# First Q and K weight slices issued by GpSimd, and the first K tile split into a head of 128 tokens and a rest of 384

## The chip, the cores and the metric

The kernel runs on one core of one Trainium2 chip. The metric is the device time of one execution in microseconds (us). A core has five engines with queues of their own: PE (matmul), DVE (vector), ACT (scalar), POOL (GpSimd) and SP (sync, which here issues most DMAs). Each works through its queue in order and waits on semaphores that other engines, or landed DMAs, raise.

## The reference

A self-attention block and a bilinear gated feed-forward block read the same input x (2048 tokens of 512), and a gate of each token mixes the two results. Inputs and output are bf16.

```python
g = sigmoid((x * gate_w).sum(-1, keepdims=True))
q, k, v = split_heads(x @ wqkv)              # 32 heads of 16
p = softmax(q @ k.T * 16 ** -0.5)            # 2048 x 2048 for each head
a = merge_heads(p @ v) @ wo
b = ((x @ w_gate) * (x @ w_up)) @ w_down     # inner width 1376
out = g * a + (1 - g) * b
```

## The kernel before

The whole program is written out as straight code: about 21,000 instructions, no loops on the chip. While it is built, a small model of the engines (`K`, with durations and latencies written into the source) is run as an event simulation; what each model engine picks next becomes the fixed order of that engine's queue on the chip. The list `P.ops` holds the resulting operations with their dependences, and `P.emit` turns these into semaphore waits. A string of digits, `ORDER`, overrides some choices. The model's times set the order alone; on the chip each engine goes through its list as the semaphores allow.

Work is tiled by 512 tokens and by blocks of 128 features (four blocks `b`, each of 8 heads). A column matmul (`mm_col`, L422 to L429, profile line L427) takes 128 input features by 32 output features, on one of four column groups of the array, against 512 moving columns; a tile of 128 x 512 takes four steps over the features times four groups, sixteen matmuls, into one bank of PSUM (`ps[:, bank, :]`, eight banks of 512 columns). Banks 0 to 6 are handed out freely; bank 7 (`OB`) belongs to the PV product, the sum of probabilities times values, and before that to the six warm-up matmuls on zeros (L389).

What matters here is the start, in the order of the queues:

- Loads (`load`, L352 to L376, profile line L354). SP and ACT issue two pieces of the first 512 tokens of x each (`PT<-in_A_x`), then SP the Q weights of the first 128 features (`wq0`, into `wq`) and ACT the K weights of the same (`wk0`, into `wa`, whose first part is `wk`); each slice is 128 KB in runs of 256 bytes. SP goes on with the V weights (`wv`, also in `wa`, 512 KB) and with twelve transposing DMAs that bring the other 1536 tokens of x into `xT`.
- POOL first fills the columns of ones in `V0` (L411), the tails of the weight tiles (L412 to L414), zeros QE (L415, after the constant `sel` of DVE) and does one integer add (L416).
- PE transposes the four x pieces (tiles x0 to x3, L465); DVE (L477) and ACT (L475) copy them in turn into `xT`.
- PE then makes tile q00 (Q of the first 512 tokens, block 0) and tile k00 (K of the same), and the V tiles of 128 tokens each (`mk_v`).
- Evacuation: q00 goes to `QE` by DVE in two operations, L507 for the even heads and L510 for the odd ones, which waits for K's copy; k00 is copied to `KK` by ACT (L487); V tiles by DVE (L555).
- A score burst (`burst`, profile line L910) is up to four row matmuls, one unit each: 128 keys of one head against 512 queries. Its dependences are the banks, Q's evacuation and the K tile that holds its keys (L887).
- ACT takes the exponential of up to three banks at once (L1008). For up to 6 of the 16 key blocks DVE and POOL do a bit-level exponential instead (L1043, L1093). PE multiplies the results by V into bank 7 (`pv_pack`, L1143); the first pack of a group also waits for what `pv_rel[0]` names, the release of that bank, empty at the start (L789).

The lines that the change and the prediction touch:

```python
359  load("sp", "wq0", wq[:, :, 0:128], wcol(0, 128), lat=4500)
360  load("act", "wk0", wk[:, :, 0:128], wcol(D, D + 128), lat=4500)
361  load("sp", "wv", wv, wcol(2 * D, 3 * D), lat=5200)
427  r = pe.matmul(ps[32 * i : 32 * i + 32, bank, :], w, x_, start=s0, stop=s1,
428                tile_position=(0, 32 * i), skip_group_check=True)
484  dst = KK[:, b, ch * 512 : (ch + 1) * 512]
486  if (b, ch) == (0, 0):
487      K.task("act", [last], lambda a: a.activation(dst, ps[:, bank, :], ACT.Copy), ...)
491  x_ = lambda kt: xT[:, kt, ch * 512 : (ch + 1) * 512]
789  pv_rel = [[]]
887  part_deps.append(bank_rel[bank] + q_ready(m) + [ev_k[b, kt // 4]])
```

Of the kernel before, what the change touches and what calls it, by code (L numbers as in the profile page):

```python
# [14 lines left out]
ACT = mybir.ActivationFunctionType  # L15
# [237 lines left out]
S, D, H, Dh, F = 2048, 512, 32, 16, 1376  # L253
T, KD, NCH, NB, FT = 16, 4, 4, 4, 11
# [7 lines left out]
OB = 7  # L262
# [27 lines left out]
def _build(nc, A_x, A_wqkv, A_wo, W_gate, W_up, W_down, gate_w, out):  # L290
# [8 lines left out]
    with ExitStack() as stack:  # L299

        def sb(name, shape, dt):
            return stack.enter_context(nc.sbuf_tensor(name, shape, dt))

        xT = sb("xT", [128, KD, S], BF16)
        wa = sb("wa", [128, FT * 512], BF16)
        wk = wa[:, 0:2048].rearrange("p (k n) -> p k n", k=KD)
# [4 lines left out]
        wq = sb("wq", [128, KD, D], BF16)  # L311
# [4 lines left out]
        KK = sb("KK", [128, NB, S], BF16)  # L316
# [24 lines left out]
        ps = stack.enter_context(nc.psum_tensor("ps", [128, 8, 512], F32))  # L341
        xr = PT[:, NC - 4 : NC, :]

        P = _Plan()
        K = _Clock(P)
# [3 lines left out]
        wcol = lambda lo, hi: A_wqkv[:, lo:hi].rearrange("(kt p) n -> p kt n", p=128)  # L349
        ld = {}  # L350

        def load(eng, key, dst, src, deps=(), lat=2500.0, **kw):  # L352
            pr = kw.pop("prio", 5)
            K.task(eng, list(deps), lambda e: e.dma_start(dst, src, **kw), 480.0, lat, lambda o: None, pr, "d" + key, 16,  # L354
                   begun=lambda o: ld.__setitem__(key, o))

        for t in range(4):
            load(("sp", "act")[t % 2], f"x0{t}", xr[:, t, :], x2[t * 128 : (t + 1) * 128, :], lat=2900)
        load("sp", "wq0", wq[:, :, 0:128], wcol(0, 128), lat=4500)
        load("act", "wk0", wk[:, :, 0:128], wcol(D, D + 128), lat=4500)  # L360
        load("sp", "wv", wv, wcol(2 * D, 3 * D), lat=5200)
        t_x = {}
        for ch in range(1, NCH):
# [23 lines left out]
        for i in range(6):  # L387
            K.task("pe", lambda: [c["pt0"]] if "pt0" in c else None,
                   lambda pe: pe.matmul(ps[:, OB, :], PT[:, 0, 0:128], PT[:, 0, :], start=True, stop=True), 427.0, 630.0, None, 0,  # L389
                   begun=lambda o: pt_first.append(o), gate=(lambda: not any(tl.name[0] == "x" for tl in tiles)) if i > 4 else None)  # L390
# [28 lines left out]
        def wcols(w, kt, c0, rhs):  # L419
            return (w[:, kt, c0 : c0 + 128], rhs)  # L420

        def mm_col(pe, bank, piece, s0, s1):  # L422
            r = None
            lhs, rhs = piece
            for i in range(4):
                w, x_ = (lhs, rhs[i]) if isinstance(rhs, list) else (lhs[:, 32 * i : 32 * i + 32], rhs)
                r = pe.matmul(ps[32 * i : 32 * i + 32, bank, :], w, x_, start=s0, stop=s1,  # L427
                              tile_position=(0, 32 * i), skip_group_check=True)
            return r  # L429

        def mm_row(pe, bank, piece, q, s0, s1):
            lhs, rhs = piece
            return pe.matmul(ps[:, bank, :], lhs[32 * q : 32 * q + 32, :], rhs[32 * q : 32 * q + 32, :], start=s0, stop=s1,  # L433
                             tile_position=(32 * q, 0), skip_group_check=True)

        ev_x, ev_k, ev_v, ev_vs, ev_q, ev_z, ev_h, ev_ot = {}, {}, {}, {}, {}, {}, {}, {}
        last_k, last_v, last_z = {}, {}, {}
        bank_rel = {b_: [] for b_ in range(8)}
# [6 lines left out]
        def xdep(ch):  # L445
            if ch == 0:
                return [ev_x.get(t) for t in range(4)]
            return [ld.get(f"x{ch}{kt}") for kt in range(KD)]

        def have(l):  # L450
            return l if all(o is not None for o in l) else None

        def give(bank, ops, hard=-1e9):
            bank_rel[bank] = ops
            bank_hard[bank] = hard
            pool_free.append(bank)
            if bank in fill_bank:
                fill_bank.remove(bank)
                fill_n[0] -= 1
# [21 lines left out]
        def mk_k(b, ch, due):  # L481
            def evac(bank, last):
                last_k[b, ch] = last
                dst = KK[:, b, ch * 512 : (ch + 1) * 512]
                reg = lambda o: ev_k.__setitem__((b, ch), o)
                if (b, ch) == (0, 0):
                    K.task("act", [last], lambda a: a.activation(dst, ps[:, bank, :], ACT.Copy), 480.0, 610.0, lambda o: give(bank, [o]), 1, begun=reg)  # L487
                else:
                    K.task("dve", [last], lambda v: v.tensor_copy(dst, ps[:, bank, :]), 600.0, 690.0, lambda o: give(bank, [o]), 2, begun=reg)

            x_ = lambda kt: xT[:, kt, ch * 512 : (ch + 1) * 512]
            return _Tile(f"k{b}{ch}", [wcols(wk, kt, b * 128, x_(kt)) for kt in range(KD)],
                         lambda: have([ld.get("wk0" if b == 0 else "wk1")] + xdep(ch)), evac, due)

# [234 lines left out]
        for t in range(4):  # L729
            tiles.append(mk_x(t))  # L730
        tiles += [mk_q(0, 0, -9), mk_k(0, 0, -9)]
        for ch in range(4):
            if ch:
                tiles.append(mk_k(0, ch, 16 * ch - 16))
            tiles += [mk_v(t, 4 * t - 8) for t in range(4 * ch, 4 * ch + 4)]
        seq = []
        for b in range(1, NB):
            lo, hi = 128 * b - 64, 128 * b - 4
            seq += [(mk_q, (0, b), lo)] + [(mk_k, (b, ch), lo + (hi - lo) * (ch + 1) // 5) for ch in range(NCH)]
            if b == 1:  # L740
                seq += [(mk_z, (), hi)]
# [20 lines left out]
        def info(m):  # L762
            return m // 8, (m % 8) // 2, m % 2
# [22 lines left out]
        pv_last = {}  # L786
        pvm = [0]
        pv_open = [True]
        pv_rel = [[]]  # L789
        mode, second = [None], [False]  # L790
        scored_n = {}

        def q_ready(m):
            cq, b, p = info(m)
            d = ev_q.get((cq, b, p))
            return d if d and all(K.ready(o) for o in d) else None
# [64 lines left out]
        def burst(picks, late=False):  # L861
            part_deps = []
# [19 lines left out]
            for k_, (who, u) in enumerate(picks):  # L882
                m, kt, j = u
                cq, b, p = info(m)
                bank = abk.pop(0) if who == "a" else lone.pop(0)
                pool_free.remove(bank)
                part_deps.append(bank_rel[bank] + q_ready(m) + [ev_k[b, kt // 4]])  # L887
                todo.append((who, u, bank))
                (act_u if who == "a" else dve_u).remove(u)
                (act_out if who == "a" else dve_out)[0] += 1  # L890
                scored_n[m] = scored_n.get(m, 0) + 1

            qt = quarter({u[2] for _, u in picks})
            if qt is not None:
                tl, kq, q = qt
# [51 lines left out]
        def pe_issue(md, fn, deps, cost, done=None, share=None, add=0.0):  # L947
            sw = SWITCH if mode[0] not in (None, md) else SECOND if second[0] else 0.0
            second[0] = mode[0] not in (None, md)
            mode[0] = md  # L950
            cost, extra = cost + add, add
            if K.now < COLD:
                cost, extra = cost * 1.8, extra + 245.0
            o = K.issue("pe", fn, deps, cost + sw, MML + sw + extra, done)
            o.work = share or MM
            return o
# [335 lines left out]
        def fill_begin(tl):  # L1292
            got = sorted(avail("col"))
            tl.bank = min(got, key=lambda x: (x - 1 in got) + (x + 1 in got))
            pool_free.remove(tl.bank)
            fill_n[0] += 1
            return bank_rel[tl.bank]

        def fill_end(tl, o):
            if not tl.todo and tl.part is None:  # L1300
                tiles.remove(tl)
                fill_bank.add(tl.bank)
                tl.evac(tl.bank, o)

        def run_fill(tl):
            deps = tl.deps()
            if tl.bank is None:
                deps = deps + fill_begin(tl)
            k, n, bank = tl.todo.pop(0), len(tl.pieces), tl.bank
            fn = tl.pieces[k]  # L1310
            s0, s1 = not tl.begun, not tl.todo and tl.part is None
            tl.begun = True
            if tl.mode == "full":
                o = pe_issue(tl.mode, lambda pe: fn(pe, bank, s0, s1), deps, tl.cost)
            else:
                o = pe_issue(tl.mode, lambda pe: mm_col(pe, bank, fn, s0, s1), deps, tl.cost)
            if hasattr(tl, "mark"):
                tl.mark(tl, o)
            fill_end(tl, o)

        def pe_step():
# [47 lines left out]
            if code == "b":  # L1369
                burst(picks)  # L1370
            elif code == "l":
                burst(later, True)
            elif code in "xy":
                burst(other[code])
            elif code == "f":
                run_fill(tl)
            elif code == "p":
                pv_pack(pv)
            elif code == "s":
                solo(sl)  # L1380
# [120 lines left out]
        P.op("sp", lambda e: e.nop(), outs)  # L1501
        if False:
            print("model", K.now, {k: round(v) for k, v in K.busy.items()}, stat)
        P.ahead = {"pe": 60, "sp": 250}
        P.emit(nc, stack, False)

# [132 lines left out]
```

## Time and profile before

| what | value |
|---|---|
| three executions | 645.26, 645.44 and 648.53 us; median 645.44 |
| profiled execution | span 643.6 us from the first to the last instruction; its own time is not listed, so the span stands 1.8 us under the median |
| busy in the span | PE 99%, ACT 97%, DVE 94%, POOL 86% |
| granted TensorE clock | 1.000 |
| first column matmul of Q | at 6.87 us |
| first scores | at 9.79 us |
| first exponential | at 10.24 us |

How to read it: the chain of work that ended last, followed back from the last instruction, tells which waits set the end. An engine that is idle elsewhere costs nothing. Times in the rows are us from the start of the span. A DMA's row shows how long its issue took; when its data lands stands in the table of DMA issues.

### The profile page before, as it was taken

The numbers are of one execution on the slowest core, as the hardware profiler recorded it, in microseconds if no ns is written. First come the engines' busy times: TensorE is split into PE (matmuls) and PEld (weight loads), VectorE is DVE, ScalarE is ACT, GpSimd is POOL, SyncE is SP. The second block draws the span as 40 slices with busy tenths as digits, with TensorE's granted clock in tenths as the row PEclk, the third lists the DMA queues.
The fourth block names the chain that finished last, engine by engine and source line by source line (L and its number), as shares of the span: only waits on it lengthen the run. The fifth ranks groups of instructions, "written<-read, shape, count | busy, mean of one in ns | idle before, by whom it ended". The sixth has DMA issues, their size and how long they took to land.

```text
span 643.6 us, 21192 instructions
## 1 busy us (share of the span) xinstructions
PE 637.1 (99%) x8729; PEld 191.8 (30%) x8729; DVE 602.5 (94%) x1021; ACT 621.7 (97%) x753; POOL 553.6 (86%) x1431
## 2 busy tenths in 40 slices
PE   8999999999999999999999999999999999999997
PEld 3332322222223232222322222332222222322233
DVE  6999999999999999999998999999998999999986
ACT  5899999999999999999999999999999999999993
POOL 2669899998998999898889999988898999899882
PEclk9999999999999999999999999999999999999999
DMA  8930201000010100101010010100001010000101
GB/s 151 287 101 15 66 10 41 2 14 26 3 36 10 39 15 16 32 1 35 5 30 16 16 40 10 31 8 12 27 7 40 20 35 3 9 23 2 29 20 35
DMA packets 28658, 21.15 MB, mean 33 GB/s; under 512 B 16488, under 2 KB 24396, under 8 KB 28560
## 3 DMA queue, kind: packets, MB, share of 16 engines
q1 hardware_dynamic: 27600, 19.26, 11.7%
q8 instruction: 68, 1.11, 0.8%
q10 hardware_dynamic: 960, 0.52, 0.3%
q14 instruction: 30, 0.25, 0.1%
HBM read 11.63 MB, written 2.37 MB: 22 GB/s over the span
## 4 chain that ended last, share of the span: by engine, by line
PE 90%; ACT 9%; DMA 1%; DVE 0%; SPq 0%; issue 0%
PE ps L1143 32%; PE ps L427 28%; PE ps L910 26%; ACT PT L1008 9%; PE ps L433 3%; DMA wq<-in_A_wqkv_dram 1%; PE ps L1254 0%; SPq L354 0%; DVE QE L714 0%; PE ps L1446 0%; DVE fl L1441 0%; DVE cb L1451 0%
## 5 line engine op out<-in xcount | busy, mean ns | idle before, releaser
L1008 ACT ACTIVATE PT<-ps 128x1024 bf16<-128x1024 f32 (+2 forms) x743 | 615.8, 1005 | 5.2 <-PE ps L910 4.5
L1093 POOL INT64_ADD PT<-PT x1420 | 550.6, 408 | 75.1 <-DVE PT L1043 65.4
L1043 DVE TENSOR_SCALAR PT<-ps 128x512 int16<-128x512 f32 x728 | 471.3, 683 | 27.1 <-PE ps L910 15.4
L910 PE MATMUL ps<-QE,KK 32*128 32x512 bf16 x2048 | 245.0, 384 | 0.1
L1143 PE MATMUL ps<-PT,V 128*32 128x512 bf16 (+1 forms) x2048 | 232.5, 384 | 0.0
L1143 PE MATMUL ps<-PT,VS 128*32 128x512 f16 x1456 | 186.6, 383 | 0.0
L910 PEld LDWEIGHTS ps<-QE,KK 32*128 32x128 bf16 x2048 | 63.6, 91 | 230.0 <-ACT PT L1008 185.2
L1143 PEld LDWEIGHTS ps<-PT,V 128*32 128x32 bf16 x2048 | 57.7, 95 | 62.9 <-issue 49.4
L1143 PEld LDWEIGHTS ps<-PT,VS 128*32 128x32 bf16 x1456 | 45.6, 95 | 42.0 <-issue 26.6
L427 PE MATMUL ps<-xT,wg 128*32 128x512 bf16 x704 | 54.6, 383 | 0.0
L427 PE MATMUL ps<-xT,wu 128*32 128x512 bf16 x704 | 54.1, 383 | 0.0
L427 PE MATMUL ps<-wd,wa 128*32 128x512 bf16 x704 | 51.6, 382 | 0.0
L624 DVE TENSOR_TENSOR usb<-ps,omg 128x512 bf16<-128x512 f32 x44 | 29.9, 680 | 0.2
L651 DVE TENSOR_TENSOR wa<-ps,usb 128x512 bf16<-128x512 f32 x44 | 29.9, 680 | 0.1
L433 PE MATMUL ps<-wo,OT 32*128 32x512 bf16 x60 | 23.1, 384 | 0.2
L1240 DVE COPY oc<-ps 128x512 f32<-128x512 f32 x31 | 21.1, 679 | 0.0
L427 PEld LDWEIGHTS ps<-wd,wa 128*32 128x32 bf16 x704 | 14.7, 95 | 19.7 <-issue 11.9
L427 PE MATMUL ps<-xT,wa 128*32 128x512 bf16 x272 | 20.2, 382 | 0.0
L427 PE MATMUL ps<-xT,wq 128*32 128x512 bf16 x256 | 18.5, 382 | 1.4 <-DMA wq<-in_A_wqkv_dram 1.4
L427 PEld LDWEIGHTS ps<-xT,wu 128*32 128x32 bf16 x704 | 13.8, 95 | 18.9 <-issue 10.4
L427 PEld LDWEIGHTS ps<-xT,wg 128*32 128x32 bf16 x704 | 13.8, 95 | 18.7 <-issue 11.1
L427 PE MATMUL ps<-wa,xT 128*32 128x512 bf16 x256 | 17.1, 381 | 0.0
(74 smaller groups left out, 142.2 us busy)
## 6 DMA issues: line engine op xcount, KB each, us to landing
rb<-rscr SPq DMA_DIRECT2D x16, 256.0 KB
QE<-Qr SPq DMA_DIRECT2D x120, 16.0 KB, 1.8
oc<-oc SPq DMA_DIRECT2D x60, 32.0 KB, 1.9
out_dram<-ost SPq DMA_DIRECT2D x12, 128.0 KB, 1.7
wu<-in_B_w_up_dram SPq DMA_DIRECT2D x1, 1376.0 KB, 6.8
wg<-in_B_w_gate_dram SPq DMA_DIRECT2D x1, 1376.0 KB, 11.0
wd<-in_B_w_down_dram SPq DMA_DIRECT2D x1, 1280.0 KB, 14.3
wa<-in_A_wqkv_dram SPq DMA_DIRECT2D x1, 512.0 KB, 6.1
```

What stands on the lines that cost most here:

```text
L427: r = pe.matmul(ps[32 * i : 32 * i + 32, bank, :], w, x_, start=s0, stop=s1, tile_position=(0, 32 * i), skip_group_check=True)
L433: return pe.matmul(ps[:, bank, :], lhs[32 * q : 32 * q + 32, :], rhs[32 * q : 32 * q + 32, :], start=s0, stop=s1, tile_position=(32 * q, 0 ...
L624: return v.tensor_tensor(usb[:, st["s"], :], ps[:, bank, :], omg[:, cf, :], ALU.mult)
L651: return v.tensor_tensor(hT[:, f, :], ps[:, bank, :], usb[:, u_at[cf, f][0], :], ALU.mult)
L910: return lambda pe: pe.matmul(ps[:, bank, :], KK[32 * j : 32 * j + 32, b, kt * 128 : (kt + 1) * 128], QE[32 * j : 32 * j + 32, p, b, :], s ...
L1008: o = K.issue("act", lambda a: a.activation(PT[:, cs, :], ps[:, bs, :], ACT.Exp, scale=math.log(2.0) / 1024.0), deps, 63.0 + 427.0 * n, 17 ...
L1043: o = K.issue("dve", lambda v: v.tensor_scalar(PT[:, y, :].bitcast(I16), ps[:, bank, :], BIAS16, 0.0, ALU.add, ALU.max), [dep] + pt_rel[y] ...
L1093: return g.int64_add(PT[:, zl, :].bitcast(I64), PT[:, sl, :].bitcast(I64), w)
L1143: return lambda pe: pe.matmul(ps[32 * it.j : 32 * it.j + 32, OB, :], lhs, it.rhs, start=s0, stop=s1, tile_position=(0, 32 * it.j), skip_gr ...
L1240: K.task("dve", deps, lambda v: v.tensor_copy(oc[:, p, :], ps[:, OB, :]), 600.0, 690.0, done, 0)
```

## The change

The two weight slices are issued by POOL, as the first operations of its queue; SP and ACT run a no-op where they issued them. Sixteen column matmuls of 128 columns (`k_head`), ahead of q00 on PE, make K of the first 128 tokens in bank 7, and ACT copies it to `KK` (`head_out`), just ahead of its other K copy. They wait for `wk0` and the first x tile. Tile k00 then covers tokens 128 to 511 in columns 128 to 511 of its bank. Score units on the first 128 keys of block 0 wait for `head_out` instead of for the copy of k00, and the first PV pack waits for `head_out` too, for the bank. The model is not told of the head: the orders of all other operations stay as they are.

```diff
@@ -356,8 +356,10 @@
 
         for t in range(4):
             load(("sp", "act")[t % 2], f"x0{t}", xr[:, t, :], x2[t * 128 : (t + 1) * 128, :], lat=2900)
-        load("sp", "wq0", wq[:, :, 0:128], wcol(0, 128), lat=4500)
-        load("act", "wk0", wk[:, :, 0:128], wcol(D, D + 128), lat=4500)
+        for eng, key, dst, lo in (("sp", "wq0", wq, 0), ("act", "wk0", wk, D)):
+            first = P.op("pool", lambda e, dst=dst, lo=lo: e.dma_start(dst[:, :, 0:128], wcol(lo, lo + 128)), (), "d" + key, 16)
+            K.task(eng, [], lambda e: e.nop(), 480.0, 4500.0, None, 5,
+                   begun=lambda o, key=key, first=first: (setattr(first, "t1", o.t1), ld.__setitem__(key, first)))
         load("sp", "wv", wv, wcol(2 * D, 3 * D), lat=5200)
         t_x = {}
         for ch in range(1, NCH):
@@ -422,9 +424,10 @@
         def mm_col(pe, bank, piece, s0, s1):
             r = None
             lhs, rhs = piece
+            at = 0 if isinstance(rhs, list) else 512 - rhs.shape[1]
             for i in range(4):
                 w, x_ = (lhs, rhs[i]) if isinstance(rhs, list) else (lhs[:, 32 * i : 32 * i + 32], rhs)
-                r = pe.matmul(ps[32 * i : 32 * i + 32, bank, :], w, x_, start=s0, stop=s1,
+                r = pe.matmul(ps[32 * i : 32 * i + 32, bank, at:512], w, x_, start=s0, stop=s1,
                               tile_position=(0, 32 * i), skip_group_check=True)
             return r
 
@@ -433,6 +436,17 @@
             return pe.matmul(ps[:, bank, :], lhs[32 * q : 32 * q + 32, :], rhs[32 * q : 32 * q + 32, :], start=s0, stop=s1,
                              tile_position=(32 * q, 0), skip_group_check=True)
 
+        def k_head(pe):
+            r = None
+            for kt in range(KD):
+                for i in range(4):
+                    r = pe.matmul(ps[32 * i : 32 * i + 32, OB, 0:128], wk[:, kt, 32 * i : 32 * i + 32], xT[:, kt, 0:128], start=kt == 0, stop=kt == KD - 1,
+                                  tile_position=(0, 32 * i), skip_group_check=True)
+            return r
+
+        head = _Op("pe", k_head, [], "pe", 1)
+        head_out = _Op("act", lambda a: a.activation(KK[:, 0, 0:128], ps[:, OB, 0:128], ACT.Copy), [head], "act", 1)
+        k_first = {}
         ev_x, ev_k, ev_v, ev_vs, ev_q, ev_z, ev_h, ev_ot = {}, {}, {}, {}, {}, {}, {}, {}
         last_k, last_v, last_z = {}, {}, {}
         bank_rel = {b_: [] for b_ in range(8)}
@@ -484,11 +498,12 @@
                 dst = KK[:, b, ch * 512 : (ch + 1) * 512]
                 reg = lambda o: ev_k.__setitem__((b, ch), o)
                 if (b, ch) == (0, 0):
-                    K.task("act", [last], lambda a: a.activation(dst, ps[:, bank, :], ACT.Copy), 480.0, 610.0, lambda o: give(bank, [o]), 1, begun=reg)
+                    K.task("act", [last], lambda a: a.activation(dst[:, 128:512], ps[:, bank, 128:512], ACT.Copy), 480.0, 610.0, lambda o: give(bank, [o]), 1, begun=reg)
                 else:
                     K.task("dve", [last], lambda v: v.tensor_copy(dst, ps[:, bank, :]), 600.0, 690.0, lambda o: give(bank, [o]), 2, begun=reg)
 
-            x_ = lambda kt: xT[:, kt, ch * 512 : (ch + 1) * 512]
+            lo = 128 if (b, ch) == (0, 0) else 0
+            x_ = lambda kt: xT[:, kt, ch * 512 + lo : (ch + 1) * 512]
             return _Tile(f"k{b}{ch}", [wcols(wk, kt, b * 128, x_(kt)) for kt in range(KD)],
                          lambda: have([ld.get("wk0" if b == 0 else "wk1")] + xdep(ch)), evac, due)
 
@@ -786,7 +801,7 @@
         pv_last = {}
         pvm = [0]
         pv_open = [True]
-        pv_rel = [[]]
+        pv_rel = [[head_out]]
         mode, second = [None], [False]
         scored_n = {}
 
@@ -884,7 +899,7 @@
                 cq, b, p = info(m)
                 bank = abk.pop(0) if who == "a" else lone.pop(0)
                 pool_free.remove(bank)
-                part_deps.append(bank_rel[bank] + q_ready(m) + [ev_k[b, kt // 4]])
+                part_deps.append(bank_rel[bank] + q_ready(m) + [ev_k[b, kt // 4] if (b, kt) != (0, 0) else head_out])
                 todo.append((who, u, bank))
                 (act_u if who == "a" else dve_u).remove(u)
                 (act_out if who == "a" else dve_out)[0] += 1
@@ -1314,6 +1329,8 @@
                 o = pe_issue(tl.mode, lambda pe: fn(pe, bank, s0, s1), deps, tl.cost)
             else:
                 o = pe_issue(tl.mode, lambda pe: mm_col(pe, bank, fn, s0, s1), deps, tl.cost)
+            if tl.name in ("q00", "k00"):
+                k_first.setdefault(tl.name, o)
             if hasattr(tl, "mark"):
                 tl.mark(tl, o)
             fill_end(tl, o)
@@ -1501,6 +1518,12 @@
         P.op("sp", lambda e: e.nop(), outs)
         if False:
             print("model", K.now, {k: round(v) for k, v in K.busy.items()}, stat)
+        head.deps = [ld["wk0"], ev_x[0]]
+        P.ops.insert(P.ops.index(k_first["q00"]), head)
+        P.ops.insert(P.ops.index(ev_k[0, 0]), head_out)
+        P.nstream.clear()
+        for o in P.ops:
+            P.nstream[o.stream] = o.seq = P.nstream.get(o.stream, 0) + 1
         P.ahead = {"pe": 60, "sp": 250}
         P.emit(nc, stack, False)
```

## The prediction

> **What bounds the kernel now.** I read the page first (shares of the engines, the chain that ended last), then the chain in order of time over the first 16 us, then the timeline of that stretch engine by engine, and last the table of DMA issues of the first 30 us.
>
> ```profile
> span 643.6 us, 21192 instructions
> PE 637.1 (99%) x8729; PEld 191.8 (30%) x8729; DVE 602.5 (94%) x1021; ACT 621.7 (97%) x753; POOL 553.6 (86%) x1431
> PE 90%; ACT 9%; DMA 1%; DVE 0%; SPq 0%; issue 0%
> ```
>
> PE is busy for 99% of the span and holds 90% of the chain that ended last. The change touches one short place, the start, where the chain in order of time (start, us, what) reads:
>
> ```profile
> 1.66 5.08 DMA wq<-in_A_wqkv_dram
> 6.73 0.14 issue
> 6.87 2.99 PE ps L427 x52
> 9.86 0.33 PE ps L910 x4
> 10.19 1.62 PE ps L427 x28
> ```
>
> The kernel waits for the first Q weight slice, issued at 1.66 and landed at 6.73. From 6.87 on PE does 52 column matmuls, four score matmuls, and goes on without a pause. The timeline shows who stands where (start, us, engine, line, operation, count, [idle before it <- what ended that]):
>
> ```profile
> 0.73 0.58 POOL L411 MEMSET V<- 128x256 bf16 x2 [0.29 <-POOLq L1624]
> 0.73 0.88 SPq L354 DMA_DIRECT2D PT<-in_A_x_dram  x2
> 1.64 0.31 POOL L414 MEMSET wd<- 32x256 f32 x1
> 1.66 0.43 SPq L354 DMA_DIRECT2D wq<-in_A_wqkv_dram  x1
> 1.67 0.46 ACTq L354 DMA_DIRECT2D wa<-in_A_wqkv_dram  x1
> 2.13 0.51 SPq L354 DMA_DIRECT2D wa<-in_A_wqkv_dram  x1
> 3.61 1.66 PE L465 MATMUL ps<-idn,PT 128*128 128x128 bf16 x16
> 3.79 0.29 DVE L406 TENSOR_SCALAR sel<-sel,rb 128x128 f32<-128x128 f32 x1
> 4.13 1.38 POOL L415 MEMSET QE<- 128x1536 f32 x1 [2.18 <-DVE sel L406]
> 4.66 1.24 ACT L475 ACTIVATE xT<-ps 128x512 bf16<-128x512 bf16 x2 [1.01 <-PE ps L465]
> 5.11 0.38 PE L389 MATMUL ps<-PT 128*128 128x512 bf16 x1
> 6.84 0.58 PEld L427 LDWEIGHTS ps<-xT,wq 128*32 128x32 bf16 x16 [1.69 <-issue]
> 6.87 1.05 PE L427 MATMUL ps<-xT,wq 128*32 128x512 bf16 x16 [1.39 <-DMA wq<-in_A_wqkv_dram]
> 7.73 1.05 PE L427 MATMUL ps<-xT,wa 128*32 128x512 bf16 x16
> 8.59 1.26 PE L427 MATMUL ps<-wa,xT 128*32 128x512 bf16 x20
> 8.83 0.60 ACT L487 ACTIVATE KK<-ps 128x512 bf16<-128x512 f32 x1 [2.92 <-PE ps L427]
> 9.79 0.39 PE L910 MATMUL ps<-QE,KK 32*128 32x512 bf16 x4
> 10.24 3.06 ACT L1008 ACTIVATE PT<-ps 128x1536 bf16<-128x1536 f32 x4 [0.81 <-PE ps L910]
> 11.74 0.40 PE L910 MATMUL ps<-QE,KK 32*128 32x512 bf16 x4
> ```
>
> Three things to see. PE stands idle for 1.39 us before 6.87, for the wq slice and nothing else: the transposed x is complete at 4.66 + 1.24 = 5.90. The 16 matmuls of Q, the 16 of K and the 20 of V follow with starts 0.86 us apart per sixteen. And the first scores do not wait for K: K is in SBUF at 8.83 + 0.60 = 9.43, the scores start at 9.79, when the V matmuls ahead of them on PE end (8.59 + 1.26 = 9.85). Landing times (last number, us after the issue):
>
> ```profile
> wa<-in_A_wqkv_dram SPq DMA_DIRECT2D x1, 512.0 KB, 6.1
> PT<-in_A_x_dram SPq DMA_DIRECT2D x2, 128.0 KB, 2.8
> wq<-in_A_wqkv_dram SPq DMA_DIRECT2D x1, 128.0 KB, 5.1
> wa<-in_A_wqkv_dram ACTq DMA_DIRECT2D x1, 128.0 KB, 5.3
> ```
>
> So wq lands at 6.7, wk at about 7.0, wv (512 KB) at 2.13 + 6.1 = 8.23, just ahead of its use at 8.59.
>
> **Two weight issues move to POOL.** They stand first in its queue, at 0.73, where the memset of V stands now; SP and ACT each run a no-op where they issued. The trace has no DMA issued by POOL, so its price is bounded. Low end: it issues as SP does, 0.43 us each, the second starting at 1.16, and the data lands like a lightly queued x piece, 2.8 us later: wk at 4.0. High end: POOL gets to its descriptors only when DVE's constants are done (4.08, the sel row), with the full 5.3 us behind it: 9.4. I take the nearest row, the same slice issued by ACT: 1.16 + 5.3 = 6.46 for wk, and 0.73 + 5.1 = 5.83 for wq.
>
> [...]
>
> What the two issues push back on POOL: the ones in V (needed by the first copy of V), three memsets of weight tails, the zeroing of QE and the first integer add. Cover: POOL waits 2.18 us for sel before the QE memset, so issues of up to 1.09 us each move nothing. Behind that it is idle until the first real add:
>
> ```profile
> 10.12 0.68 DVE L555 CAST V<-ps 128x512 bf16<-128x512 f32 x1
> 13.53 0.77 POOL L1093 INT64_ADD PT<-PT  x2 [7.68 <-DVE PT L1043]
> ```
>
> Together 2.18 + 7.68 = 9.9 us for two issues. The ones are due at 10.12 and are written at 1.31 now, 8.8 us of slack. Only issues of over 4.4 us each would reach DVE, and then each further microsecond costs one.
>
> SP's later work comes 0.43 + 0.04 us earlier: wv issued at 1.66 lands at about 7.76 by its own 6.1 us, and the twelve DMA transposes of the rest of x move up with it. ACT's issue ends 0.46 us earlier, ahead of a table load that is done long before x is copied. Neither is on the path as it stands; wv becomes it if Q starts early.
>
> The x pieces now share the DMA engines with the weight slices from the start. How full those are:
>
> ```profile
> 2.00:3.00 1.00, 1.00 (x4) 0.30 (x2) 0.83 (x8) 0.84 (x1) 0.00 (x0) 1.00 0.89 253
> 3.00:4.00 1.00, 0.89 (x7) 0.42 (x6) 0.84 (x11) 0.64 (x2) 0.00 (x0) 1.00 1.00 311
> ```
>
> The last two columns are the share of the engines' time and GB/s. At 311 GB/s a 128 KB slice takes 0.42 us, so x comes 0 to 0.4 us later per slice that gets ahead of it; I take 0.2, and xT is complete at 6.1. That is hidden as long as wk lands later than that, as taken.
>
> **The K head.** Sixteen matmuls of 128 columns, ahead of Q on PE, waiting for wk and the first x tile. This is an added wait: behind it on PE stands everything, Q first, which before needed only wq. Columns are conserved (K's tile shrinks from 512 to 384), so the streaming time only moves; what is added is sixteen weight loads and their pace. Q's sixteen loads start within 0.58 us where PE was not yet limiting, 36 ns each: I take 0.58 us for the head. Low end 0, if wk lands before xT is complete and the head runs inside that wait; high end the present 0.86 us per sixteen.
>
> The narrower K tile: 0.86 x 128/512 = 0.22 us less on PE (low end 0 if weight loads set the pace).
>
> **The head's copy on ACT**: 128 columns, at most the 0.60 us of the present 512-column copy; K's remaining copy shrinks. ACT stands idle 2.92 us before K's copy and 0.81 before the first exponential. The copy runs under Q's matmuls: nothing, and at worst 0.6 less K's saving if the head ran so late that both copies meet.
>
> **Releasing the first scores on the head instead of on K**: nothing, for PE reaches them at 9.79 and K was there at 9.43. Behind them ACT has K's other copy ahead of the first exponential in its own queue anyway.
>
> **The values' bank**: the first PV pack now also waits for the head's copy. That comes at 14.24, the copy is over by about 8:
>
> ```profile
> 14.24 0.60 PE L1143 MATMUL ps<-PT,V 128*32 128x512 bf16 x7
> ```
>
> **The sum.** wk lands 6.46; PE starts 0.14 later, as now, 6.60; head 0.58: Q at 7.18 against 6.87, +0.31. K is 0.22 shorter: V at 8.68 against 8.59, +0.09, and wv at 7.76 is no hindrance. From there the same instructions in the same order, with PE 90% of the chain, so the shift carries to the end nearly one for one: span 643.7. The span lies 1.8 us under the median of 645.44, and nothing of the change lies outside it but the issue's start: 645.5. The three times span 645.26 to 648.53, 0.5%, so 0.5% (3.2 us) is about what a measurement can tell from no change.
>
> **Rivals.**
>
> *Weights early.* wk lands between 4.0 and 6.1; the head vanishes in the wait for x; Q starts at about 6.2. Then K ends at 6.2 + 0.86 + 0.64 = 7.7 and V starts when wv is there, 7.76: 0.83 us ahead of 8.59. Time 644.6. For it: PE's 1.39 us of idle is weight wait alone, and POOL could issue 0.9 us before SP does. Against it: the DMA engines are full from 2 to 4 us, so an earlier issue mostly reorders the same bytes.
>
> *Late descriptors.* DVE is 0.83 and 0.84 busy in the rows of 2 to 4 us, on the constants that end at 4.08. If POOL cannot write descriptors beside it, wk lands at 6.8 to 9.4; Q starts at wk + 0.72, which is 7.5 to 10.1, and V 0.4 to 3.0 us later than now: 645.9 to 648.5, middle 647. Against it: POOL's memsets at 0.73 to 1.95 ran beside busy DVE rows. [...]
>
> *A slow first DMA on POOL* (the other side). If POOL's first DMA carries a start-up of t before its first descriptor, Q moves by all of t: PE has no other work. From t = 3.1 us on the kernel is slower by over 0.5%. The wait would also let PE cool:
>
> ```profile
> L389 PE MATMUL ps<-PT x6: 379/634/634, 1.2 to 5.1; 128*128 128x512 bf16 x6
> ```
>
> These are the warm-up matmuls, 634 ns until 5 us of the span and 379 then. With t = 5 us and four microseconds at 634 instead of 379 ns (1.6 us lost), the time is 652. Against it: POOL's first integer add, at 5.66, starts without any start-up in the trace.
>
> *The change does nothing* falls within my forecast: the head and the narrower K cancel, and the weights land when the full DMA engines allow.
>
> **How the numbers follow.** Forecast as summed 0.45 (645.5, with 0.5 either way for x, head and copy); early weights 0.28; late descriptors 0.20; slow start 0.05; 0.02 for a median that falls on a run like the 648.53. The likeliest is 645.5. The range takes in the early case with its low end (644.6 less the 0.6 by which wv could come early, 644.0) and most of the late one (to 647.5), leaving out about 0.15. Only the slow start and a stray median are past +0.5%, for the late case ends at 3.0 us: slower 0.07; no case gives 3.2 us, the whole of the wait being 1.39: faster 0.02; the same 0.91.
>
> **What the next profile would show.** Right: in the chain the first piece is the DMA of wa (wk) from POOL, landing near 6.5; sixteen 128-column matmuls on a line of their own ahead of Q; Q near 7.2, V near 8.7, the first scores 0.1 from 9.79. Early: the chain's start is x (PT, xT), then the DMA of wv; Q near 6.2. Late: Q after 7.5 and the issue of the first descriptors behind DVE's constants. Wrong would be a Q start that moves without V moving, or a later stage that waits where it did not: then the shift does not carry.

## The result, and the profile after

The changed kernel takes 652.06 us (median of six executions, 650.88 to 652.67) against 646.83 for the kernel before beside it (645.26 to 648.53): ratio 1.0082, 95% interval 1.0064 to 1.010. It is 5.2 us slower. The forecast was 645.5, no change, in a range of 644.0 to 647.5.

The clock row of the kernel before, and then the page of the changed kernel:

```profile
PEclk9999999999999999999999999999999999999999
```

```profile
span 649.0 us, 21226 instructions
PE 639.2 (98%) x8745; PEld 192.7 (30%) x8745; DVE 603.6 (93%) x1021; ACT 621.8 (96%) x754; POOL 555.2 (86%) x1433
PEclk7999999999999999999999999999999999999999
...
q0 software_dynamic: 96, 0.26, 0.3%
PE 86%; ACT 9%; DVE 2%; DMA 2%; SPq 0%; issue 0%; POOL 0%; DVEq 0%; POOLq 0%
```

PE is busy 2.1 us longer (DVE 1.1, ACT 0.1), and the first slice of the clock row has fallen from 9 to 7 tenths. The rest of the added 5.4 us is waiting: PE holds 98% of the span instead of 99%. A new queue, q0, carries POOL's two slices. The chain in order of time over the first 16 us shows the place:

```profile
1.27 1.06 POOL wq L360
2.34 0.01 issue
2.35 6.87 DMA wa<-in_A_wqkv_dram
9.22 0.14 issue
9.35 0.62 PE ps L443 x16
9.97 4.84 PE ps L430 x48
14.82 0.33 PE ps L925 x4
```

The K slice is issued at 2.35, lands at 9.22, and the 48 column matmuls that took 2.99 us for 52 before now take 4.84. The timeline of PE, where L443 is the head, L430 the old L427 and L925 the old L910:

```profile
4.76 0.38 PE L391 MATMUL ps<-PT 128*128 128x512 bf16 x1
9.35 0.62 PE L443 MATMUL ps<-xT,wa 128*32 128x128 bf16 x16 [4.21 <-DMA wa<-in_A_wqkv_dram]
9.73 1.95 PE L430 MATMUL ps<-xT,wq 128*32 128x512 bf16 x16
11.44 1.52 PE L430 MATMUL ps<-xT,wa 128*32 128x384 bf16 x16
12.72 2.10 PE L430 MATMUL ps<-wa,xT 128*32 128x512 bf16 x20
14.75 0.39 PE L925 MATMUL ps<-QE,KK 32*128 32x512 bf16 x4
```

PE waits 4.21 us instead of 1.39. Q begins 1.71 us before K where it was 0.86. The stretches by the microsecond (length, then busy PE, PEld, DVE, ACT, POOL, granted clock, DMA share, GB/s; the DMA share, which can pass 1, isn't used here) say why: the granted clock falls to a half during the wait and stays there until Q, K and V are nearly done.

```profile
6.00:7.00 1.00, 0.00 (x0) 0.00 (x0) 0.00 (x0) 0.00 (x0) 0.18 (x1) 1.00 1.67 211
7.00:8.00 1.00, 0.00 (x0) 0.00 (x0) 0.00 (x0) 0.00 (x0) 0.00 (x0) 0.79 0.51 97
8.00:9.00 1.00, 0.00 (x0) 0.00 (x0) 0.00 (x0) 0.00 (x0) 0.00 (x0) 0.50 1.23 211
13.00:14.00 1.00, 1.00 (x13) 0.37 (x8) 0.47 (x1) 0.49 (x1) 0.00 (x0) 0.50 0.62 143
14.00:15.00 1.00, 1.00 (x16) 0.28 (x8) 0.63 (x2) 0.00 (x0) 0.00 (x0) 0.80 0.65 32
```

By its places the delay of the first scores is 14.75 - 9.79 = 4.96 us: 2.49 because the slice that PE waits for lands at 9.22 instead of 6.73; 0.37 for the head; 2.10 because Q to scores takes 14.75 - 9.73 = 5.02 instead of 9.79 - 6.87 = 2.92, although K is narrower. The span grew by 5.4. The remaining 0.4 came later: after 20 us PE waits twice for DVE's exponentials here, 0.3 and 0.2 us, and before it never did. In this trace the clock fell in PE's wait of 4.21 us (0.50 from 8 to 14 us), and in the kernel before it did not fall in the wait of 1.39 (1.00 through Q, K and V). The record has the fall at 7.58, 2.4 us after PE's last matmul ended (5.14). It has three changes in the first 20 us, up at 4.16, down at 7.58 and up at 14.40, that is 3.4 and 6.8 us apart.

### The profile page after: what moved, and what is told of

Same layout as the page of the kernel before. It is cut to its first block, busy times and chain, and to the rows that moved or that the text cites. A ratio compares the mean times of both kernels' runs of the same rounds, so it can differ in the third digit from the quotient of the medians.

```text
span 649.0 us, 21226 instructions
## 1 busy us (share of the span) xinstructions
PE 639.2 (98%) x8745; PEld 192.7 (30%) x8745; DVE 603.6 (93%) x1021; ACT 621.8 (96%) x754; POOL 555.2 (86%) x1433
## 2 busy tenths in 40 slices
DMA packets 27698, 21.15 MB, mean 33 GB/s; under 512 B 15464, under 2 KB 23372, under 8 KB 27600
## 3 DMA queue, kind: packets, MB, share of 16 engines
q1 hardware_dynamic: 27072, 19.13, 10.6%
## 4 chain that ended last, share of the span: by engine, by line
PE 86%; ACT 9%; DVE 2%; DMA 2%; SPq 0%; issue 0%; POOL 0%; DVEq 0%; POOLq 0%
PE ps L1158 31%; PE ps L430 27%; PE ps L925 25%; ACT PT L1023 9%; PE ps L436 3%; DVE PT L1058 1%; DMA wa<-in_A_wqkv_dram 1%; DMA rb<-rscr 1%; SPq L539 0%; SPq L1211 0%; POOL wq L360 0%; PE ps L1269 0%; DVE OT L1237 0%; SPq L1243 0%; DVE QE L729 0%
## 5 line engine op out<-in xcount | busy, mean ns | idle before, releaser
L925 PE MATMUL ps<-QE,KK 32*128 32x512 bf16 x2048 | 245.1, 384 | 0.3 <-DVE PT L1058 0.2
L925 PEld LDWEIGHTS ps<-QE,KK 32*128 32x128 bf16 x2048 | 63.5, 91 | 230.4 <-ACT PT L1023 184.2
L430 PE MATMUL ps<-xT,wg 128*32 128x512 bf16 x704 | 54.6, 383 | 0.3 <-DVE PT L1058 0.3
L430 PE MATMUL ps<-xT,wu 128*32 128x512 bf16 x704 | 54.1, 383 | 0.0
L430 PE MATMUL ps<-wd,wa 128*32 128x512 bf16 x704 | 51.5, 382 | 0.0
L430 PE MATMUL ps<-xT,wa 128*32 128x512 bf16 (+1 forms) x272 | 20.6, 391 | 0.0
L430 PEld LDWEIGHTS ps<-wd,wa 128*32 128x32 bf16 x704 | 14.8, 95 | 19.5 <-issue 11.9
L430 PEld LDWEIGHTS ps<-xT,wg 128*32 128x32 bf16 x704 | 13.8, 95 | 19.1 <-issue 11.1
L430 PEld LDWEIGHTS ps<-xT,wu 128*32 128x32 bf16 x704 | 13.8, 95 | 18.9 <-issue 10.4
L430 PE MATMUL ps<-xT,wq 128*32 128x512 bf16 x256 | 19.4, 398 | 0.0
L430 PE MATMUL ps<-wa,xT 128*32 128x512 bf16 x256 | 17.9, 396 | 0.0
```

Source lines behind the costliest of these rows:

```text
L430: r = pe.matmul(ps[32 * i : 32 * i + 32, bank, at:512], w, x_, start=s0, stop=s1, tile_position=(0, 32 * i), skip_group_check=True)
L925: return lambda pe: pe.matmul(ps[:, bank, :], KK[32 * j : 32 * j + 32, b, kt * 128 : (kt + 1) * 128], QE[32 * j : 32 * j + 32, p, b, :], s ...
```

## The experiments

What they had to tell apart: whether the loss lies in the weights' landing, in the clock, or in the K head; and why the slices land late, by a latency of POOL's own queue or by what shares the DMA engines.

### The two halves alone

The kernel before with only the slices moved to POOL, no head:

```diff
- load("sp", "wq0", wq[:, :, 0:128], wcol(0, 128), lat=4500)
- load("act", "wk0", wk[:, :, 0:128], wcol(D, D + 128), lat=4500)
+ for eng, key, dst, lo in (("sp", "wq0", wq, 0), ("act", "wk0", wk, D)):
+     first = P.op("pool", lambda e, dst=dst, lo=lo: e.dma_start(dst[:, :, 0:128], wcol(lo, lo + 128)), (), "d" + key, 16)
...
```

> The kernel before with only the two weight slices moved to POOL, no K head. Theory (the weights' late landing and the fallen clock make the loss): wq lands near 8.1 as in the changed kernel, Q starts near 8.2 (6.87 before), the first scores come between 11.1 (clock kept) and 13.2 (clock halved) against 9.79, so the time is 1.3 to 3.4 us over before. Rival (the K head and its wait make the loss): Q starts near 6.9 and the time is that of before, within 0.5 us.

Measured: 650.32 us against 645.79, ratio 1.0062 (1.0048 to 1.0077), 4.5 us between the medians where I had expected 1.3 to 3.4. The chain of its profile:

```profile
1.27 7.64 DMA wq<-in_A_wqkv_dram
9.04 5.56 PE ps L429 x39
```

The slice wq lands at 8.91, Q starts at 9.04, the granted clock is 0.50 from 8 us on, and the first scores stand at 14.53, later than both of my bounds. The profiled execution took 654.37, the longest of the four; the others took 649.17 to 651.29. The slices without the head make most of the loss.

Only the head, the slices issued by SP and ACT as before:

```diff
- first = P.op("pool", lambda e, dst=dst, lo=lo: e.dma_start(dst[:, :, 0:128], wcol(lo, lo + 128)), (), "d" + key, 16)
...
+ load("sp", "wq0", wq[:, :, 0:128], wcol(0, 128), lat=4500)
+ load("act", "wk0", wk[:, :, 0:128], wcol(D, D + 128), lat=4500)
```

> The changed kernel with the two weight slices issued by SP and ACT as before; the K head stays. Theory: the head starts with wk at about 7.1, Q follows 0.4 later at 7.5, K is 0.2 shorter, first scores near 10.2 against 9.79 and the time 0.4 us over before, less than the runs scatter. Rival (the head costs most of the loss): first scores after 12 and 3 us or more over before.

Measured: 647.19 against 645.79, ratio 1.0016 (1.0003 to 1.0030), 1.4 us between the medians where I had expected 0.4; executions from 645.18 to 650.77. In the profiled one, which took 650.77 and is the longest of the twelve, wk landed at 7.51, the first scores came at 12.07 and the matmuls of Q ran slow, as PE's timeline shows:

```profile
5.32 0.63 PE L389 MATMUL ps<-PT 128*128 128x512 bf16 x1
7.65 0.62 PE L441 MATMUL ps<-xT,wa 128*32 128x128 bf16 x16 [1.69 <-DMA wa<-in_A_wqkv_dram]
8.03 1.95 PE L428 MATMUL ps<-xT,wq 128*32 128x512 bf16 x16
```

Here the last warm-up matmul still took 0.63 us (0.38 in the kernel before): the clock was low from the beginning and had not risen. The windows of the profile read 1.00 there only because the record of the clock begins with its first change, which in this trace is the rise, at 10.73; in the kernel before it is at 4.91. Six executions took 645.18 to 646.69, as before; the other six took 647.68 to 650.77, against one of 17 over 647 in the kernel before. Three of those six have a mean granted clock of 0.997 and three, the profiled one among them, of 1.000, which after a late rise says nothing. That all six are slow by the clock is likely and not shown. The head alone is a small loss on average.

### The clock

Matmuls on zeros fill PE's wait ahead of the head, 18 and then 14 of them:

```diff
+ P.ops.insert(P.ops.index(k_first["q00"]), _Op("pe", idle_fill, [c["pt0"]], "pe", 1))
```

> The changed kernel with 18 more matmuls on zeros (512 columns, into the values' bank) on PE ahead of the K head, which fill about 3.9 of the 4.2 us of PE's wait. Theory: the granted clock stays at 1.00, Q, K and V run at 379 ns a matmul, the first scores come near 12.5 instead of 14.75 and the time is 2.2 us under the changed kernel, 3 us over before. Rival (the half clock is a label of the wait and no price of its own): first scores near 14.7 and no gain.

Measured: 649.86, ratio 1.0066 (1.0051 to 1.0080), 4.1 us over before instead of 3; first scores at 12.77, Q's sixteen matmuls at full speed (1.03 us). The fill ended at 9.9, about a microsecond after wk's landing, and delayed the head.

> The changed kernel with 14 matmuls on zeros ahead of the K head (18 ran past the landing in the earlier run, so that the head came 0.9 us late). Theory (the half clock has a price of its own, 2 us): the head starts with wk near 9.0, first scores near 12, the time 2 us under the changed kernel and 3 to 3.5 over before. Rival (the price is the landing alone): within 0.7 us of the changed kernel.

> The changed kernel once more, on the chip of the three kernels beside it. Both theories: 5 to 6.5 us over before; POOL's wk lands between 8.5 and 10.7, the clock falls to a half during the wait.

Measured on one chip: the changed kernel 652.78, ratio 1.0082 (1.0054 to 1.011), 4.9 us over before, wk landing at 10.25; with 14 matmuls 651.66, ratio 1.0055 (1.0026 to 1.0083). PE in the profile of the latter:

```profile
9.98 0.41 PE L443 MATMUL ps<-xT,wa 128*32 128x128 bf16 x16 [0.98 <-DMA wa<-in_A_wqkv_dram]
10.20 1.05 PE L430 MATMUL ps<-xT,wq 128*32 128x512 bf16 x16
11.06 0.84 PE L430 MATMUL ps<-xT,wa 128*32 128x384 bf16 x16
11.71 1.26 PE L430 MATMUL ps<-wa,xT 128*32 128x512 bf16 x20
12.91 0.39 PE L925 MATMUL ps<-QE,KK 32*128 32x512 bf16 x4
```

Q to scores takes 2.71 us here, 4.64 in the changed kernel's profile beside it and 5.02 in its first: 1.9 and 2.3 us are the clock's in these profiles. In the times the gain is unclear, 1.1 us between the medians with intervals that overlap, between what the theory and the rival say. The profiled execution (649.76) is the shortest of four; two of the other three (651.47 to 651.92) have a mean granted clock of 0.997, so the filler probably doesn't always hold the clock, which no profile shows.

### Why the slices land late

Three kernels take away, one by one, what shares the DMA engines with POOL's slices. First wv and everything behind it in SP's queue:

```diff
+ ld["wv"].deps.append(ld["wk0"])
```

> The changed kernel, but SP issues wv and everything behind it (the transposing DMAs too) only when POOL's K slice has landed; only x and the two slices share the DMA engines. Theory (contention: POOL's packets stand behind wv and the transposes): wk lands at 6.5 or earlier. Rival (POOL's queue has a latency of its own): wk lands at 8.5 to 9.3 as in the changed kernel. The kernel as a whole gets slower either way, since wv comes later; only the landing counts.

Then the transposing DMAs alone:

```diff
+ ld["x10"].deps.append(ld["wk0"])
```

> The changed kernel; SP issues wv as there, and holds only the transposing DMAs until wk has landed. If the transposes are what POOL's packets stand behind: wk lands near 6 as with wv held too (5.75). If wv is: wk still lands after 8. If both share it: near 7, with wv landed before 7.5.

Then all of SP's and ACT's traffic, x too:

```diff
+ for key in ("x00", "x01"):
+     ld[key].deps.append(ld["wk0"])
```

> The changed kernel, but SP and ACT issue nothing (not even x) before POOL's wk has landed, so that the two slices have the DMA engines to themselves. It measures POOL's own latency. Theory (own latency is small, the rest is shared engines): wk lands 2.5 to 3.4 us after its issue at 2.35, against 3.4 beside x and 6.9 to 7.9 in the changed kernel. Rival (a fixed price of POOL's queue): 4 us or more. The kernel as a whole comes out some 4 us slower, since x is late; only the landing counts.

The K slice is issued at 2.35 in each. Its rows in the tables of DMA issues (last number, us to landing), in the order alone, beside x, beside x and wv, and in the changed kernel beside all:

```profile
wa<-in_A_wqkv_dram POOLq DMA_DIRECT2D x1, 128.0 KB, 2.8
```

```profile
wa<-in_A_wqkv_dram POOLq DMA_DIRECT2D x1, 128.0 KB, 3.4
```

```profile
wa<-in_A_wqkv_dram POOLq DMA_DIRECT2D x1, 128.0 KB, 5.3
```

```profile
wa<-in_A_wqkv_dram POOLq DMA_DIRECT2D x1, 128.0 KB, 6.9
```

So POOL's own latency is 2.8 us, x adds 0.6, wv 1.9 and the transposes 1.6, each from one profile. With all of the traffic the same row reads 6.5 and 7.5 in the kernels with 18 and 14 fillers and 7.9 in the repeat, so the last step lies between 1.2 and 2.6. The theory of contention holds, and of my three answers for the transposes "both share it" is the nearest, although wk landed at 7.6, later than the 7 that I wrote, and wv at 8.27 instead of before 7.5. With the slices in time PE was in order at once: with wv held, the head started at 5.88 and Q at 6.10, all at the full clock (0.41 and 1.05 us for sixteen). Single executions of these: 647.78, 650.92 and 651.13 us, each paying for what it holds back; with wv held, V waits 2.12 us for it.

What the slices lost is their place ahead of wv and the transposes, and the rows say that it is a place in time more than in a queue. In the kernel before, wk stood in ACT's queue, beside SP's and not ahead of it, but it was issued at 1.67, ahead of wv (2.13) and of the first transpose (2.69); in the changed kernel it is issued at 2.35, behind both (1.67 and 2.15). The tables of DMA packets by the microsecond fit: from 3 to 4 us POOL's queue moved 0.07 MB with wv held, and nothing in the changed kernel, where the packets of SP's queue (q1) took 55% and those of ACT's (q10) 40% of the sixteen engines' time. And transposes that SP issues after POOL's slices did not slow them in the kernels below: wk landed 3.3 us after its issue with transposes issued from 4.30 on, 3.4 with them held until wk. No run moves the slices' issue in time and nothing else, so time and queue are not cleanly separated.

### Restoring the order

If that is so, wv belongs behind the slices in the same queue. POOL issues wv third, and SP's transposes wait for wk:

```diff
- load("sp", "wv", wv, wcol(2 * D, 3 * D), lat=5200)
+ third = P.op("pool", lambda e: e.dma_start(wv, wcol(2 * D, 3 * D)), (), "dwv", 16)
+ ld["x10"].deps.append(ld["wk0"])
```

> The changed kernel, but wv is issued by POOL too, third behind wq and wk, and SP starts its transposing DMAs when wk has landed. Theory (what ran ahead of the slices was SP's traffic in another queue; in one queue the order holds): wk lands near 5.8, Q starts near 6.2, wv lands near 7.6, first scores near 9.0 against 9.79, the time within 1 us of before. Rival (POOL's queue is slow for any data): wv lands after 9.5, first scores after 11 and 1.5 us or more over before.

Measured: 646.69 against 647.92, ratio 0.9992 (0.9961 to 1.0022), the same. Head and V ran as the theory said, but a later wait gave it back:

```profile
5.87 0.41 PE L444 MATMUL ps<-xT,wa 128*32 128x128 bf16 x16 [0.84 <-DMA wa<-in_A_wqkv_dram]
6.09 1.05 PE L431 MATMUL ps<-xT,wq 128*32 128x512 bf16 x16
...
9.15 0.39 PE L926 MATMUL ps<-QE,KK 32*128 32x512 bf16 x4
...
13.88 1.05 PE L431 MATMUL ps<-xT,wa 128*32 128x512 bf16 x16 [1.08 <-ACT PT L1024]
```

The row at 13.88 is K of the second 512 tokens, which needs the first four transposes. It is put down to ACT; but the fourth transpose, issued at 9.6 (7.2 before), landed 4.1 us later, at about 13.7, and in the next kernel the same K matmuls start before that ACT operation does (12.90 and 13.02). There the transposes wait for the last x piece (`x03`), start at 4.30, the fourth has landed by 12.5 and the wait is gone:

> All three weight pieces in POOL's queue, in the order wq, wk, wv, and SP's transposing DMAs held only until the last x piece has landed (near 3.8) instead of until wk (5.75). Theory: wk lands near 6, Q near 6.3, first scores near 9.3 (9.79 before), and K of the second 512 tokens no longer waits for its transposes, so the time is 0.3 to 0.6 us under before. Rival (the transposes catch up with the slices again): wk after 7, first scores after 10, 0.5 us or more over before.

> The kernel with all three weight pieces in POOL's queue and the transposes held until x has landed, once more, on the chip of its two variants: 0.3 to 1.2 us under before, and scattering less than before.

Measured: 645.51 against 646.34, ratio 0.9985 (0.9974 to 0.9996), and on another chip 645.63 against 646.07, ratio 0.9989 (0.9978 to 1.0000). It beats both kernels; the kernel before by 0.8 and 0.4 us between the medians, with the second interval just reaching no change. It scattered less in the first set (645.03 to 646.25 against 644.99 to 649.29) and hardly less in the second (644.96 to 647.54 against 645.15 to 648.01). In the first profile POOL's wk lands 3.3 us after its issue, with SP's transposes issued from 4.30 on in the other queue, while it is under way. PE there:

```profile
6.19 1.31 PE L431 MATMUL ps<-xT,wq 128*32 128x512 bf16 x16
7.32 0.83 PE L431 MATMUL ps<-xT,wa 128*32 128x384 bf16 x16
8.13 1.26 PE L431 MATMUL ps<-wa,xT 128*32 128x512 bf16 x20
9.32 0.39 PE L926 MATMUL ps<-QE,KK 32*128 32x512 bf16 x4
...
12.90 1.05 PE L431 MATMUL ps<-xT,wa 128*32 128x512 bf16 x16
```

The same without the K head:

> The same, without the K head (K of the first 512 tokens in one tile, as before). Theory (the head is neither the loss nor a gain): Q starts when x is complete, near 6.2, first scores near 9.3 and the time within 0.4 us of the kernel with the head. Rival (the head lets the scores start early): 0.5 us or more slower without it.

Measured: 645.64, ratio 0.9989 (0.9980 to 0.9997), first scores at 9.06 as in the profile with the head beside it. The head is worth nothing here: with the weights in time Q starts when x is complete (5.69 without the head), and V starts at 7.87 with the head and without it, where it waits 0.27 us for wv.

And with its six warm-up matmuls cut to 32 columns:

> The kernel with all three weight pieces in POOL's queue, but its six warm-up matmuls on zeros are cut from 512 columns to 32, so PE is nearly idle until the transposes. The weights land as before, near 6. Theory (the low clock alone costs some 2 us): Q, K and V run at 634 ns a matmul for 3 to 4 us, first scores near 11.3 instead of 9.3, the time 1.5 to 2.5 us over the same kernel with its warm-up. Rival (the low clock goes along with late weights and costs nothing itself): first scores near 9.3 and the same time within 0.5 us.

Measured: 646.20 against 645.63 with the warm-up, ratio to before 1.0001 (0.9991 to 1.0011). I had expected 1.5 to 2.5 us: a miss. Its profile shows the transposes at the low clock as in the other (1.86 us for sixteen in both), Q's sixteen matmuls partly slow (1.54 us), K at full speed (0.83), first scores at 9.31. By the clock's record the rise comes at 7.10, and at 6.37 and 6.73 in the two profiles with the warm-up, all within a microsecond of Q's start, so this kernel never made the cold stretch that it was meant to price.

### Two edits without POOL

SP and ACT issue the slices between their x pieces:

```diff
+ for wkey, xkey in (("wq0", "x02"), ("wk0", "x03")):
+     P.ops.remove(ld[wkey])
+     P.ops.insert(P.ops.index(ld[xkey]), ld[wkey])
```

> The kernel before, nothing on POOL and no head: SP issues wq and ACT wk between their two x pieces instead of behind them. Theory (in a queue the order of issue is the order of landing): wq and wk land 0.4 us earlier, the last x pieces 0.4 later, both near 6.4; first scores near 9.5, the time 0.3 us under before. Rival (their ends are set by the traffic of the other queues): no change of the first scores beyond 0.1 us.

Measured: 649.38 against 646.34, ratio 1.0042 (1.0026 to 1.0057): a miss. The chain's start and PE:

```profile
1.67 4.95 DMA PT<-in_A_x_dram
6.67 0.61 PE ps L465 x4
7.27 0.43 PE ps L389
8.01 4.96 PE ps L427 x48
```

The slice wq now lands 3.1 us after its issue (4.3 of the span) and wk 3.6 (4.8), far ahead of the 6.4 that I wrote, but the last two x pieces take 4.3 and 4.9 where they took 2.8 and 3.2. The pieces that are issued behind are now the late ones; and PE, with its transposes later, did Q (1.90 us for sixteen matmuls), K (1.95) and a part of V at the low clock, which rose at 12.04. The first scores came at 12.90.

SP's transposes wait for the last x piece, nothing else changed:

```diff
+ ld["x10"].deps.append(ld["x03"])
```

> The kernel before, but SP's transposing DMAs wait until the last x piece has landed. Theory (the transposes slow the end of the weight slices): wq lands up to 0.8 us earlier, near 6.0, first scores near 9.2 and the time 0.3 to 0.6 us under before, if K of the second 512 tokens does not wait for its transposes. Rival (wq stands ahead of them in SP's queue anyway): wq still lands near 6.7 and the time is that of before.

Measured: 646.39 against 646.34, ratio 1.0004 (0.9992 to 1.0016); wq lands 5.3 us after its issue (5.1 before), the first scores come at 10.02. The rival is right: in SP's queue wq stands ahead of the transposes anyway.

## Why the prediction was wrong

The step that failed is the landing of wk, taken as 1.16 + 5.3 = 6.46 and measured at 9.22. It has two parts. I let POOL issue at 0.73 and 0.43 us each, as SP does; POOL's first DMA starts at 1.27 and takes 1.06, the second 0.76:

```profile
1.27 1.06 POOL L360 DMA_DIRECT2D wq<-in_A_wqkv_dram  x1 [0.82 <-POOLq L1647]
2.35 0.76 POOL L360 DMA_DIRECT2D wa<-in_A_wqkv_dram  x1
3.10 0.60 POOL L413 MEMSET V<- 128x256 bf16 x2
```

That is 2.35 instead of 1.16, and 1.2 us of the 2.8. The other 1.6 are the landing: I carried the 5.3 us over from ACT's row as if it belonged to the slice; it belonged to the slice's place ahead of SP's later work. SP in the kernel before, where wv follows at 2.13, and in the changed one:

```profile
2.69 11.27 SPq L354 DMA_TRANSPOSE xT<-in_A_x_dram  x8
```

```profile
1.67 0.43 SPq L354 DMA_DIRECT2D wa<-in_A_wqkv_dram  x1
2.15 10.95 SPq L354 DMA_TRANSPOSE xT<-in_A_x_dram  x8
```

Taking wq out of SP's queue let wv and the transposes start half a microsecond earlier, and POOL's late issue put wk behind them; the landing took 6.87. I had booked that earlier start as a gain without a cost. The x pieces, which I feared for, were not slowed (2.8 and 3.0 us). The high end of my bounds, 9.4, held, but for the wrong reason: POOL's two issues were over at 3.10 with DVE 84% busy beside them (from 1 to 3 us), and with the DMA engines to themselves the slices landed in 3.0 and 2.8 us, so the rival of late descriptors was not at work; that they could wait for DVE was an assumption of mine, which no run shows.

The second term missing from the sum is the clock, 2.1 us at the first scores. I priced it only under the rival of a slow first DMA, at 1.6 us, and gave that 0.05. That rival comes nearest to what happened, in its size and in the cooling, but only in a small part in its mechanism: POOL's first issue starts 0.5 us later and lasts 0.6 us longer than I took, while the DMA behind it alone lands in 3.0 us. That its time, 652, is the measured one is luck: it was made of a start-up of 5 us, which no run shows. The rival of early weights describes the kernels with the order restored (Q from 5.7 on, V waiting for wv in two of them); in the two best it was worth 0.4 to 0.8 us, where it was priced at 0.8.

Point by point on the rest. The head: taken as 0.58 us, it delays Q by 0.38 at the low clock and by 0.22 at the full one (5.88 to 6.10 with wv held). The narrower K tile: 0.22 less, measured 0.86 to 0.65 (8.82 to 9.47 with the transposes held), right. POOL's memsets behind the issues: covered, as said; the zeroing of QE starts at 4.54 instead of 4.13, released by DVE's sel. The scores released on the head: nothing, right, for K's rest was copied by 13.50 and the scores came at 14.75, behind V. The values' bank: no wait seen. wv: landed at about 7.97 and kept nobody. The shift: carried to the end, 4.96 us at the first scores and 5.4 in the span. The time around the span: I set 1.8 us against the median; the changed kernel's profiled execution took 651.96 for its span of 649.0, 2.96, and the executions of the kernel before beside the experiments took 2.65 to 3.22 us more than their spans. So the span of 643.6 stood for 646.2 to 646.8, and the sum was 1 us short on that account alone.

## What to carry to other kernels

Here a transfer's time to landing went with what had been issued ahead of it, in the other queues (POOL's K slice: 2.8 us alone, 6.9 behind x, wv and the transposes) and in its own (the last x pieces: 4.3 and 4.9 us behind the slices, 2.8 and 3.2 ahead of them). So before moving an issue to an idle engine, list what stood behind it and will now run ahead of it or beside it, and move those along. Where PE waits for the first load, ask how long it then stands idle: waits of 4.0 us and more (4.03, 4.21 and 5.12) were paid a second time here, in the clock, at 0.50; waits of 1.4 and 1.9 us were not, but a kernel whose clock had not risen before a wait of 1.7 us did Q slowly too. A row's duration may be borrowed for a moved operation only if its neighbours move too: ACT's 5.3 us for this slice was 6.9 on POOL.

## What the hardware showed that was not expected

- A DMA of 128 KB in runs of 256 bytes took POOL 1.06 us for the first and 0.76 for the second, against 0.43 to 0.46 on SP and ACT; and POOL's first starts at 1.27, where SP's first is issued at 0.75.
- POOL's 256 KB went as 96 packets, where the same two slices had been 528 packets each in the queues of SP and ACT (their counts fell from 27600 to 27072 and from 960 to 432); with the engines to itself a slice lands in 2.8 to 3.0 us.
- The granted clock reads 1.00 over stretches in which warm-up matmuls take 0.63 us, since its record begins with the first change; the low clock at the start is seen in durations only. That first rise came anywhere from 4.0 us (all three weights in POOL's queue, transposes held until wk) to 13.2 us (the slices alone), and after it the clock fell in three profiles, each time 3.4 us later (4.16 and 7.58 in the changed kernel).
- Six warm-up matmuls of 512 columns were worth 0.6 us between the medians once the weights came in time, which the scatter doesn't tell from nothing.
